# Second layer's tiles in the order in which the first layer ends; output copies one place later; the first pair's weight parts inside the last expert

## The chip, the core and the metric

The kernel runs on one core of a Trainium2 chip. The metric is the device time of one execution in microseconds. Engines: PE (TensorE: matmuls; its weight loads are listed as PEld), DVE (VectorE), ACT (ScalarE), POOL (GpSimd) and SP (SyncE, which here only issues transfers). A PE matmul accumulates into a bank of PSUM, and DVE or ACT reads the bank afterwards.

## The reference, cut

Three stages follow each other: a linear attention with decay (`_attn_ref`), a mixture of eight experts of which each token takes one (`_moe_ref`), and a two-layer perceptron with an ELU between (`_moe2_ref`). The change lies in the last stage and at its border to the second one:

```
def _moe2_ref(x, w_in, w_out):              # x: 2304 x 512, w_in: 512 x 2048, w_out: 2048 x 512
    h = x @ w_in
    g = np.where(h > 0.0, h, np.exp(np.minimum(h, 0.0)) - 1.0)
    return (g @ w_out).astype(np.float32)
```

## The kernel before, in words

Every operand of a matmul is split into a high part (a rounded copy, made on ACT) and a low part (the difference, made on DVE), and `three` (L223 to L229) issues three matmuls for a product: high by high, high by low, low by high.

**The experts.** The loop `for i in range(NI1 + 1)` runs 8 experts by 8 hidden tiles; `mm1` makes a hidden tile, `mm2` one step later adds it to four output banks, and after an expert's last tile the four banks are copied to `y` (three copies on ACT, the fourth on DVE). `decode` steps prepare the perceptron's weights in the gaps, and `load_pair` loads them in pairs. After the loop stand `decode(99)`, the allocation of the tiles for the perceptron's weights (`awt`, one set for even and one for odd groups) and, for the first pair, `weights_high` (ACT) and `weights_low` (DVE) of its four quarters `A11`, `A12`, `A21`, `A22`: four casts and four differences of 128x256. Then comes a `tc.If` for experts with too many tokens, whose body is not entered with these inputs, and then the perceptron.

**The perceptron.** The tokens are cut into three blocks of 768 (`TB`), the 2048 hidden units into eight pairs of 128-wide rows; a group `g` in 0 to 23 is one pair on one block. Groups 0 to 7 (`plain`) have four places with two products each; groups 8 to 23 (`seven`) compute the same with seven products (Strassen's way), one at each of seven places, with sums on DVE in between. A product is six matmuls of 384 columns into one of two banks. The group's four quarters (j, s) of the first layer (j: which 128 hidden units, s: which half of the block) end in the order (0,0) at place 2, (1,1) at 4, (1,0) at 5, (0,1) at 6. Each then goes through `elu`: three ACT operations (`r`, `ex`, `r`), one place later two on DVE (`ex`, L1220 and L1221), one place after that the high part `gh` on ACT, and one after that the low part `gl` on DVE (both L1224). So `gl` of (1,0) falls at place 1 of the next group.

**The second layer.** `out_units(g)` is a generator of twelve units for group g, which are issued during group g + 1, after the products: a unit is the three matmuls of 512 columns for token tile t (0 to 5) and hidden half j (0 or 1). Tiles t = 0 to 2 read the half s = 0, t = 3 to 5 the half s = 1. The list `share` says how many units follow each product: none at place 0, two at each of places 1 to 6 (in group 23 fewer, with the rest at the end). After a tile's last unit in the last pair of a block, its bank is copied to `ob` (tag `tsum`, three buffers; even t on ACT, odd t on DVE) and POOL scatters the rows to the output with an indirect transfer.

**What sets the order.** The program runs with a manual schedule: each engine executes in the order in which the code issues. At each place the order is: the product, `elus(2, ..)` (`gl`), `elus(0, 1)` (the two DVE steps), the queued tasks `low` and `high`, `elus(1, ..)` (`gh`), then the sum or copy of the place, then the units. At place 0 ACT copies the product's bank to `u` (L1308), and the product of place 2 adds to that same bank. The weights of groups 8 to 23 come back from DRAM through POOL's queue: `out_move(g, True)` (four loads for the second layer, tags with two free buffers) and then `weights_load(g + 1)` (seven loads for the first), both issued at place 0 of group g.

Of the kernel before, what the change touches and what calls it, by code (L numbers as in the profile page):

```python
# [9 lines left out]
F32 = mybir.dt.float32  # L10
# [69 lines left out]
def tile_kernel(ctx: ExitStack, tc: tile.TileContext, q, k, v, emb, tau, w1, w2, w_in, w_out, const, out):  # L80
# [932 lines left out]
    for low in lows + [xpose(0, 2)]:  # L1013
        low()
    NI1 = NE * 8
    load_unit(1, nc.scalar)
    split(1)
    for i in range(NI1 + 1):
# [28 lines left out]
        if i < NI1 - 2:  # L1047
            decode(2)

    decode(99)  # L1050

    awt = [[], []]
    for j in range(2):
        t = dec.tile([P, 2, 2, 2, P], F32R, tag="draw", name=f"awd{j}")
        awt[0] += [t[:, 0], t[:, 1]]
    for nm in ("dsq", "db1"):
        awt[0] += [dec.tile([P, 2, 2, P], F32R, tag=nm, name=f"aw{nm}{j}", bufs=2) for j in range(2)]
    t = raw.tile([P, 4, 2, 2, P], F32R, tag="rawb", name="awr")
    awt[1] += [t[:, i] for i in range(4)]
    awt[1] += [spl.tile([P, 2, 2, P], F32R, tag=nm, name=f"aw{nm}") for nm in ("ah", "al", "bh", "bl")]  # L1060
    A11, A12, A21, A22, S1, S2, S3, S4 = range(8)
    t = raw.tile([P, 2, 4, 2, P], F32, tag="rawb", name="sums")
    sums = [{i: t[:, g, k] for k, i in enumerate((S1, S2, S3, S4))} for g in range(2)]
    wsd = [dr.tile([P, 8, 2 * 2 * P], F32R, name=f"wsd{g}") for g in range(8)]
    wbd = [dr.tile([P, 4, DM], F32R, name=f"wbd{g}") for g in range(8)]

    def weights_src(g, i):
        if i >= S1:
            return sums[g % 2][i]
        ra = pairs[g][:, 0]  # L1070
        return ra[:, i % 2 * 2:i % 2 * 2 + 2, i // 2 * P:i // 2 * P + P]

    def weights_sum(g, i):
        x = lambda k: weights_src(g, k)
        p_, q_, op = {S1: (A21, A22, ALU.add), S2: (S1, A11, ALU.subtract), S3: (A11, A21, ALU.subtract), S4: (A12, S2, ALU.subtract)}[i]
        vec.tensor_tensor(out=x(i), in0=x(p_), in1=x(q_), op=op)

    def weights_high(g, i):
        nc.scalar.copy(out=awt[g % 2][i][:, 0], in_=weights_src(g, i))

    def weights_low(g, i):
        w = awt[g % 2][i]
        vec.tensor_tensor(out=w[:, 1], in0=weights_src(g, i), in1=w[:, 0].bitcast(F32), op=ALU.subtract)
# [9 lines left out]
    for i in (A11, A12, A21, A22):  # L1093
        weights_high(0, i)
        weights_low(0, i)
# [338 lines left out]
```

## Time and profile before

| | us |
|---|---|
| median of three runs | 802.85 |
| the three runs | 800.53, 802.85, 803.28 |
| the profiled execution, its own time | 804.02 |
| span of the profiled execution, first to last instruction | 801.9 |
| PE busy in the span | 747.2 (93%) |
| DVE busy | 542.3 (68%) |
| ACT busy | 439.2 (55%) |
| POOL busy | 277.0 (35%) |

The profiled execution took 804.02 us, of which 2.12 us lie outside its span. In the span the experts end at about 362 us, groups 0 to 7 run to about 498.6 us, groups 8 to 23 to about 775 us, and the rest is the last group's second layer and the last scatter. A row of a timeline begins with the start of the instruction in us from the span's start, then its duration; what stands in brackets at its end is the idle time of the engine before it and the instruction that ended this. A PE matmul's duration overlaps that of the next one: the distance between the starts of two matmuls is what each takes. PEclk is the granted TensorE clock, 1.00 for 2.4 GHz and 0.50 for 1.2 GHz.

### The profile page before, as it was taken

To read this page: it belongs to the slowest core of one execution; us is meant where nothing else is said; L and a number is where in the kernel's file an instruction comes from. 1 tells how busy PE (TensorE), PEld (TensorE's weight loads), DVE (VectorE), ACT (ScalarE), POOL (GpSimd) and SP (SyncE) were. 2 spreads that over 40 slices of the span, in tenths; PEclk is the share of its full clock that TensorE was granted. 3 is DMA by queue.
4 is the path that set the end of the run, shared out by engine and by line. 5 is a ranking of instruction groups with operands and counts; after the bars stand their busy time and mean duration, and the time that the engine had idled before them with its cause. 6 is when DMAs were issued, how large, how long until landed. Compare 5 with 4: busy or idle time off the path is not lost.

```text
span 801.9 us, 13886 instructions
## 1 busy us (share of the span) xinstructions
PE 747.2 (93%) x4952; PEld 675.3 (84%) x4953; DVE 542.3 (68%) x1127; ACT 439.2 (55%) x917; POOL 277.0 (35%) x460
## 2 busy tenths in 40 slices
PE   8899978999999999996999999899999899999984
PEld 7898957999999999995999899788887777888863
DVE  4366577889989999866778778555556765545551
ACT  3555534455555556547767778445445664544550
POOL 5365665269843512000000001553223445222303
PEclk9999999999999999999999999999999999999997
DMA  9898827776886877831967764786645668665512
GB/s 218 224 237 229 254 91 257 243 234 225 288 311 215 307 277 240 303 126 55 326 225 246 259 229 159 235 223 199 169 145 145 171 183 226 197 169 145 144 53 78
DMA packets 131870, 165.60 MB, mean 207 GB/s; under 512 B 63530, under 2 KB 68430, under 8 KB 131798
## 3 DMA queue, kind: packets, MB, share of 16 engines
q1 hardware_dynamic: 102630, 107.91, 41.4%
q0 software_dynamic: 27440, 54.15, 23.4%
q10 hardware_dynamic: 1728, 2.62, 1.0%
q8 instruction: 41, 0.67, 0.3%
q14 instruction: 31, 0.25, 0.1%
HBM read 123.73 MB, written 40.91 MB: 205 GB/s over the span
## 4 chain that ended last, share of the span: by engine, by line
PE 30%; DVE 9%; ACT 7%; issue 5%; POOL 1%; DMA 1%; POOLq 0%; DVEq 0%
PE o L229 6%; PE c L227 5%; PE c L228 5%; PE c L229 5%; PE o L227 5%; PE o L228 5%; DVE ex L1220 3%; ACT ex L1216 2%; ACT r L1217 2%; ACT r L1215 2%; DVE ex L1221 2%; DVE gl L1224 1%; DMA obl<-wbd 1%; DVE v L1294 1%; DVE u L1294 1%
## 5 line engine op out<-in xcount | busy, mean ns | idle before, releaser
L1220 DVE SCALAR_TENSOR_TENSOR ex<-ex,r 128x384 f32<-128x384 f32 x96 | 53.5, 558 | 123.0 <-ACT r L1217 123.0
L1201 POOL DMA_DIRECT2D oah<-wbd x16 | 8.7, 542 | 318.9 <-DMA wsd<-awdsq 185.9
L228 PE MATMUL acc<-hl,bh 128*128 128x342 f32 (+7 forms) x256 | 78.7, 308 | 2.1 <-DVE hl L869 1.8
L227 PE MATMUL h<-xth,ah 128*128 128x332 f32 (+7 forms) x252 | 78.5, 311 | 0.0
L229 PE MATMUL h<-xth,al 128*128 128x332 f32 (+7 forms) x252 | 76.7, 304 | 1.6 <-DVE al L217 1.5
L227 PE MATMUL acc<-hh,bh 128*128 128x342 f32 (+7 forms) x256 | 77.5, 303 | 0.0
L229 PE MATMUL acc<-hh,bl 128*128 128x342 f32 (+7 forms) x256 | 77.4, 302 | 0.0
L228 PE MATMUL h<-xtl,ah 128*128 128x332 f32 (+7 forms) x252 | 76.4, 303 | 0.0
L1224 ACT CAST gh<-ex 128x384 fp32r<-128x384 f32 x97 | 49.3, 508 | 33.5 <-DVE ex L1221 32.9
L229 PE MATMUL o<-obh,gl 128*128 128x512 f32 x144 | 58.5, 406 | 8.7 <-DVE gl L1224 7.2
L227 PE MATMUL o<-obh,gh 128*128 128x512 f32 x144 | 58.8, 409 | 3.3 <-ACT gh L1224 2.4
L229 PE MATMUL o<-oah,gl 128*128 128x512 f32 x144 | 57.5, 399 | 0.0
L227 PE MATMUL o<-oah,gh 128*128 128x512 f32 x144 | 57.3, 398 | 0.0
L228 PE MATMUL o<-oal,gh 128*128 128x512 f32 x144 | 57.0, 396 | 0.0
L228 PE MATMUL o<-obl,gh 128*128 128x512 f32 x144 | 56.9, 395 | 0.0
L1224 DVE TENSOR_TENSOR gl<-ex,gh 128x384 fp32r<-128x384 f32 x97 | 53.5, 552 | 1.2 <-ACT gh L1224 1.1
L1216 ACT ACTIVATE ex<-r 128x384 f32<-128x384 f32 x96 | 50.4, 525 | 3.0
L1217 ACT ACTIVATE r<-r 128x384 f32<-128x384 f32 x96 | 50.4, 525 | 3.0
L228 PEld LDWEIGHTS acc<-hl,bh 128*128 128x128 f32 x256 | 48.2, 188 | 4.4 <-DVE hl L869 4.3
L216 ACT CAST bh<-rawb 128x512 fp32r<-128x512 f32 x64 | 39.8, 622 | 19.4 <-PE acc L228 19.4
L217 DVE TENSOR_TENSOR bl<-rawb,bh 128x512 fp32r<-128x512 f32 x64 | 47.3, 739 | 3.5 <-ACT bh L216 3.4
L229 PEld LDWEIGHTS h<-xth,al 128*128 128x128 f32 x252 | 47.5, 189 | 2.4 <-DVE al L217 2.4
(408 smaller groups left out, 2182.1 us busy)
## 6 DMA issues: line engine op xcount, KB each, us to landing
rawa<-in_moe_w_dram SPq DMA_DIRECT2D x15, 1024.0 KB, 6.3
rawb<-in_moe_w_dram SPq DMA_DIRECT2D x15, 1024.0 KB
pair<-wd SPq DMA_DIRECT2D x18, 512.0 KB, 5.4
draw<-in_moe_w_in_dram SPq DMA_DIRECT2D x16, 512.0 KB, 9.0
wd<-db SPq DMA_DIRECT2D x32, 256.0 KB
draw<-in_moe_w_out_dram SPq DMA_DIRECT2D x16, 512.0 KB, 5.4
awr<-wsd POOLq DMA_DIRECT2D x24, 256.0 KB
awd<-wsd POOLq DMA_DIRECT2D x21, 256.0 KB
```

Source lines behind the costliest of these rows:

```text
L216: nc.scalar.copy(out=hi, in_=src)
L217: nc.vector.tensor_tensor(out=lo, in0=src, in1=hi.bitcast(F32), op=ALU.subtract)
L227: nc.tensor.matmul(o, lh, rh, start=first, stop=False, skip_group_check=free)
L228: nc.tensor.matmul(o, lh, rl, start=False, stop=False, skip_group_check=free)
L229: nc.tensor.matmul(o, ll, rh, start=False, stop=last, skip_group_check=free)
L1215: nc.scalar.activation(out=r, in_=c, func=AF.Relu, scale=-1.0)
L1216: nc.scalar.activation(out=ex, in_=r, func=AF.Exp, scale=-1.0)
L1217: nc.scalar.activation(out=r, in_=r, func=AF.Tanh, scale=-0.5)
L1220: vec.scalar_tensor_tensor(out=ex, in0=ex, scalar=1.0, in1=r, op0=ALU.add, op1=ALU.mult)
L1221: vec.scalar_tensor_tensor(out=ex, in0=c, scalar=0.0, in1=ex, op0=ALU.max, op1=ALU.add)
L1224: return middle, lambda: nc.scalar.copy(out=gh, in_=ex), lambda: vec.tensor_tensor(out=gl, in0=ex, in1=gh.bitcast(F32), op=ALU.subtract)
L1294: vec.tensor_tensor(out=o, in0=x, in1=c, op=ALU.add)
```

## The change

Three edits. **First**, `out_units` no longer goes tile by tile with both halves of each. It takes the units (t, 0) for t = 0, 1, 2, then (t, 1) for the same tiles, and then tiles 3 to 5 (for groups 8 to 22 all (t, 1) first and then all (t, 0); for groups 0 to 7 and 23 tile by tile). The units' number and the places with their shares stay. **Second**, the copy of a finished output tile and its scatter move out of `out_units` into `rows_out`, which is called at the next place, after `elus(0, 1)` and ahead of `low` and `high`; at the end of the program it is called after every unit. Beside it, `weights_load(g + 1)` is now issued ahead of `out_move(g, True)`. **Third**, the definitions and the first weight set move ahead of the expert loop's body, decoding is ended one step earlier, and the high and low parts of `A11`, `A12` are issued at step 62 and those of `A21`, `A22` at step 63 of the loop instead of after it.

```
-        for t in range(NTB):
+        todo = [(t, j) for j in range(2) for t in range(3)]
+        if g < 8:
+            todo += [(t, j) for t in range(3, NTB) for j in range(2)]
+        elif g < NG2 - 1:
+            todo += [(t, j) for j in (1, 0) for t in range(3, NTB)]
+        else:
+            todo += [(t, j) for t in range(3, NTB) for j in (1, 0)]
+        seen = set()
+        for t, j in todo:
             sl = slice(t * P, (t + 1) * P)
-            for j in range(2):
-                gh, gl = gs[g][j]
-                three(acc6[t], (gh[:, sl], gl[:, sl]), bs[g][j], p == 0 and j == 0, p == 7 and j == 1)
-                if p == 7 and j == 1:
-                    ob = fp.tile([P, DM], F32, tag="tsum", name=f"ob{b}_{t}", bufs=3)
...
+            gh, gl = gs[g][j]
+            three(acc6[t], (gh[:, sl], gl[:, sl]), bs[g][j], p == 0 and t not in seen, p == 7 and t in seen)
+            if p == 7 and t in seen:
+                ended.append((b, t))
+            seen.add(t)
+            yield
...
+    def rows_out():
+        for b, t in ended:
+            ob = fp.tile([P, DM], F32, tag="tsum", name=f"ob{b}_{t}", bufs=3)
...
             elus(2, 3)
             elus(0, 1)
+            rows_out()
             for f in low[k] + high[k]:
...
         put(low, o, out_tiles, g)
-        put(low, o, out_move, g, True)
         if g + 1 < NG2:
             put(low, o, weights_load, g + 1)
+        put(low, o, out_move, g, True)
...
-        if i < NI1 - 2:
+        if i < NI1 - 3:
             decode(2)
...
+        elif i == NI1 - 3:
+            decode(99)
+            first_set()
+        elif i < NI1:
+            for k in ((A11, A12), (A21, A22))[i - NI1 + 2]:
+                weights_high(0, k)
+                weights_low(0, k)
...
     for _ in out_units(NG2 - 1):
-        pass
+        rows_out()
+    rows_out()
```

What this moves is shown at three places. On PE, the units that follow the product of place 1 in group 19 (`o2_t` is the bank of token tile t of block 2, `gh18_j` and `gl18_j` the parts of the hidden half j, `oa`, `ob` the second layer's weights for j = 0 and 1); before:

```order
L227 MATMUL o2_0_8736<-oah18_8862,gh18_0_8901 128x512
L228 MATMUL o2_0_8736<-oal18_8863,gh18_0_8901 128x512
L229 MATMUL o2_0_8736<-oah18_8862,gl18_0_8902 128x512
L227 MATMUL o2_0_8736<-obh18_8864,gh18_1_8903 128x512
L228 MATMUL o2_0_8736<-obl18_8865,gh18_1_8903 128x512
L229 MATMUL o2_0_8736<-obh18_8864,gl18_1_8904 128x512
```

and with the change:

```order
L227 MATMUL o2_0_8736<-oah18_8862,gh18_0_8901 128x512
L228 MATMUL o2_0_8736<-oal18_8863,gh18_0_8901 128x512
L229 MATMUL o2_0_8736<-oah18_8862,gl18_0_8902 128x512
L227 MATMUL o2_1_8737<-oah18_8862,gh18_0_8901 128x512
L228 MATMUL o2_1_8737<-oal18_8863,gh18_0_8901 128x512
L229 MATMUL o2_1_8737<-oah18_8862,gl18_0_8902 128x512
```

The second unit at place 1 now reads the half j = 0 of tile 1; the first unit that reads the half j = 1 stands as second unit at place 2.

On DVE, the end of place 1 of group 8 and the places after it, where block 0 is copied out (`ob0_t` is the copy of output tile t); before:

```order
L1224 TENSOR_TENSOR gl7_1_7152<-ex7_11_7281,gh7_1_7151 128x384
L1241 COPY ob0_1_7380<-o0_1_6119 128x512
L1220 SCALAR_TENSOR_TENSOR ex8_00_7370<-ex8_00_7370,r8_00_7369 128x384
L1221 SCALAR_TENSOR_TENSOR ex8_00_7370<-c0_8_0_7294,ex8_00_7370 128x384
L1294 TENSOR_TENSOR v8_7297<-u8_7296,c1_8_2_7384 128x384
L1294 TENSOR_TENSOR v8_7297<-v8_7297,c0_8_3_7404 128x384
L1241 COPY ob0_3_7424<-o0_3_6121 128x512
L1224 TENSOR_TENSOR gl8_0_7366<-ex8_00_7370,gh8_0_7365 128x384
L1220 SCALAR_TENSOR_TENSOR ex8_11_7414<-ex8_11_7414,r8_11_7413 128x384
L1221 SCALAR_TENSOR_TENSOR ex8_11_7414<-v8_7297,ex8_11_7414 128x384
L1294 TENSOR_TENSOR w8_7298<-u8_7296,c1_8_2_7384 128x384
```

and with the change:

```order
L1231 TENSOR_TENSOR gl7_1_7152<-ex7_11_7281,gh7_1_7151 128x384
L1227 SCALAR_TENSOR_TENSOR ex8_00_7366<-ex8_00_7366,r8_00_7365 128x384
L1228 SCALAR_TENSOR_TENSOR ex8_00_7366<-c0_8_0_7294,ex8_00_7366 128x384
L1318 TENSOR_TENSOR v8_7297<-u8_7296,c1_8_2_7376 128x384
L1264 COPY ob0_1_7403<-o0_1_6119 128x512
L1318 TENSOR_TENSOR v8_7297<-v8_7297,c0_8_3_7396 128x384
L1231 TENSOR_TENSOR gl8_0_7362<-ex8_00_7366,gh8_0_7361 128x384
L1227 SCALAR_TENSOR_TENSOR ex8_11_7414<-ex8_11_7414,r8_11_7413 128x384
L1228 SCALAR_TENSOR_TENSOR ex8_11_7414<-v8_7297,ex8_11_7414 128x384
L1264 COPY ob0_3_7433<-o0_3_6121 128x512
L1318 TENSOR_TENSOR w8_7298<-u8_7296,c1_8_2_7376 128x384
```

The copy of tile 3 now stands behind `gl8_0` and the two DVE steps of quarter (1,1), directly ahead of the sum `w8`.

On ACT, the end of the last expert (`hh62`, `hh63` are its last two hidden tiles, `acc56_d` its output banks, `awd0`, `awd1` the tiles of the four quarters' parts); before:

```order
L868 ACTIVATE hh62_5390<-h62_5377 128x276
L868 ACTIVATE hh63_5419<-h63_5406 128x276
L891 TENSOR_LOAD offi_89
L891 ISA x2
L888 ISA
L888 COPY y_1978<-acc56_0_5196 128x276
L888 ISA
L888 COPY y_1978<-acc56_1_5197 128x276
L888 ISA
L888 COPY y_1978<-acc56_2_5198 128x276
L1079 CAST awd0_5469<-pair0_5220 128x256 x2
L1079 CAST awd1_5470<-pair0_5220 128x256 x2
```

and with the change:

```order
L868 ACTIVATE hh62_5412<-h62_5399 128x276
L1033 CAST awd0_5393<-pair0_5236 128x256 x2
L868 ACTIVATE hh63_5445<-h63_5432 128x276
L1033 CAST awd1_5394<-pair0_5236 128x256 x2
L891 TENSOR_LOAD offi_89
L891 ISA x2
L888 ISA
L888 COPY y_1978<-acc56_0_5212 128x276
L888 ISA
L888 COPY y_1978<-acc56_1_5213 128x276
L888 ISA
L888 COPY y_1978<-acc56_2_5214 128x276
```

The four casts moved from behind the last expert's copies to behind its last two hidden tiles; the four differences on DVE moved alike.

## Rows read from the trace of the kernel before

**Rows 1.** Busy time of the engines in one stretch, groups 0 to 7: stretch, length in us, busy us and instructions of PE, PEld, DVE, ACT and POOL, granted clock, share of the DMA engines, GB/s.

```profile
380.00:498.00 118.00, 117.35 (x586) 106.10 (x587) 90.66 (x195) 86.80 (x191) 0.00 (x0) 1.00 0.69 244
```

**Rows 2.** Timeline of PE: the product of place 2 of group 8; then from place 6 of group 18 to place 2 of group 19 (products of places 6, 0 and 1, the first unit, the first matmul of the second unit and its last, the product of place 2, the unit after it); then the product of place 2 of group 23.

```profile
502.22 0.34 PE L227 MATMUL c<-t1h,awd 128*128 128x384 f32 x1
...
690.03 0.34 PE L227 MATMUL c<-t2h,awdb 128*128 128x384 f32 x1
...
692.48 0.34 PE L227 MATMUL c<-t0h,awr 128*128 128x384 f32 x1
...
693.65 0.44 PE L227 MATMUL c<-t4h,awal 128*128 128x384 f32 x1
...
694.80 0.39 PE L227 MATMUL o<-oah,gh 128*128 128x512 f32 x1
...
695.73 0.50 PE L227 MATMUL o<-obh,gh 128*128 128x512 f32 x1
...
696.98 0.50 PE L229 MATMUL o<-obh,gl 128*128 128x512 f32 x1 [0.51 <-DVE gl L1224]
697.31 0.34 PE L227 MATMUL c<-t1h,awr 128*128 128x384 f32 x1
...
698.37 0.39 PE L227 MATMUL o<-oah,gh 128*128 128x512 f32 x1
...
765.58 0.34 PE L227 MATMUL c<-t1h,awr 128*128 128x384 f32 x1
```

**Rows 3.** Timelines of DVE and of ACT in the same stretch around the start of group 19: the last sum of group 18, the first DVE step of its quarter (0,1), `gl` of its quarter (1,0); and ACT's copy of the bank of group 19's place 0.

```profile
693.05 0.55 DVE L1294 TENSOR_TENSOR u<-u,c 128x384 f32<-128x384 f32 x1
695.30 0.56 DVE L1220 SCALAR_TENSOR_TENSOR ex<-ex,r 128x384 f32<-128x384 f32 x1 [1.24 <-ACT r L1217]
...
696.37 0.55 DVE L1224 TENSOR_TENSOR gl<-ex,gh 128x384 fp32r<-128x384 f32 x1
...
695.58 0.47 ACT L1308 COPY u<-c 128x384 f32<-128x384 f32 x1
```

**Rows 4.** Timelines of PE, POOL and DVE around the start of group 9: PE's product of place 6 of group 8 and of places 0, 1 and 2 of group 9; POOL's scatter of output tile 0 of block 0; DVE's copy of tile 3.

```profile
512.01 0.34 PE L227 MATMUL c<-t2h,awdb 128*128 128x384 f32 x1
...
515.63 0.44 PE L227 MATMUL c<-t0h,awr 128*128 128x384 f32 x1 [1.01 <-DVE w L1294]
...
518.95 0.69 PE L227 MATMUL c<-t4h,awal 128*128 128x384 f32 x1 [2.01 <-DVE u L1294]
...
522.98 0.34 PE L227 MATMUL c<-t1h,awr 128*128 128x384 f32 x1
...
508.52 1.05 POOL L1246 DMA_INDIRECT out_dram<-ob,idc  x1 [2.01 <-DMA awr<-wsd]
...
512.89 0.69 DVE L1241 COPY ob<-o 128x512 f32<-128x512 f32 x1 [3.96 <-DMA out_dram<-ob,idc]
```

**Rows 5.** Timelines of PE and ACT at the starts of groups 14 and 16: PE's last matmul of the second unit in group 14; in group 16 its first unit and the product of place 2, and ACT's copy of the bank of place 0.

```profile
608.85 0.50 PE L229 MATMUL o<-obh,gl 128*128 128x512 f32 x1 [1.38 <-DVE gl L1224]
...
642.57 0.39 PE L227 MATMUL o<-oah,gh 128*128 128x512 f32 x1
...
645.92 0.34 PE L227 MATMUL c<-t1h,awd 128*128 128x384 f32 x1
...
644.05 0.47 ACT L1308 COPY u<-c 128x384 f32<-128x384 f32 x1
```

**Rows 6.** Busy time in single microseconds, columns as in Rows 1: after the idle time at the start of group 0, and after that at the start of group 9.

```profile
366.00:367.00 1.00, 1.00 (x4) 1.00 (x4) 0.96 (x2) 1.00 (x2) 0.00 (x0) 0.50 0.00 0
...
519.00:520.00 1.00, 1.00 (x3) 1.00 (x4) 0.96 (x2) 0.97 (x2) 0.59 (x3) 0.50 0.16 61
```

**Rows 7.** Timelines of SP, ACT, DVE and PE from the last expert to the perceptron's first product: SP's issue of the load of the first pair's first-layer half; ACT's `hh` of the last hidden tile; DVE's copy of the fourth output bank and its four differences for the first pair; ACT's first token part; PE's first product.

```profile
343.82 0.60 SPq L179 DMA_DIRECT2D pair<-wd  x1
...
358.78 0.40 ACT L868 ACTIVATE hh<-h 128x276 fp32r<-128x276 f32 x1 [2.66 <-PE h L229]
...
361.85 0.45 DVE L886 COPY y<-acc 128x276 f32 x1 [2.20 <-PE acc L229]
362.22 1.42 DVE L1083 TENSOR_TENSOR awd<-pair,awd 128x256 fp32r<-128x256 f32 x4
364.02 0.93 ACT L1173 CAST t0h<-y 128x384 fp32r<-128x384 f32 x2 [0.94 <-DVEq L1101]
364.58 0.45 PE L227 MATMUL c<-t0h,awd 128*128 128x384 f32 x1 [2.77 <-ACT t0h L1173]
```

**Rows 8.** Timelines of PE, POOL and ACT at the end: PE's first matmul that reads the half j = 1 of group 23, the last matmul of that unit, and the last matmul of all; POOL's scatters of output tiles 0, 1 and 5 of block 2; ACT's copy of tile 4.

```profile
780.37 0.50 PE L227 MATMUL o<-obh,gh 128*128 128x512 f32 x1 [1.68 <-ACT gh L1224]
...
781.62 0.79 PE L229 MATMUL o<-obh,gl 128*128 128x512 f32 x1 [0.52 <-DVE gl L1224]
783.32 1.03 POOL L1246 DMA_INDIRECT out_dram<-ob,idc  x1 [20.64 <-ACT ob L1243]
...
785.98 1.00 POOL L1246 DMA_INDIRECT out_dram<-ob,idc  x1 [1.55 <-DVE ob L1241]
...
789.31 0.59 ACT L1243 COPY ob<-o 128x512 f32<-128x512 f32 x1 [2.21 <-PE o L229]
...
790.28 0.39 PE L229 MATMUL o<-obh,gl 128*128 128x512 f32 x1
...
791.73 0.97 POOL L1246 DMA_INDIRECT out_dram<-ob,idc  x1 [0.46 <-DVE ob L1241]
```

More of the change, by code (lines that the diff above doesn't have):

```diff
@@ L1046, in tile_kernel @@
         split(i + 2)
-        if i < NI1 - 2:
+        if i < NI1 - 3:
             decode(2)
-    decode(99)
-    awt = [[], []]
-    for j in range(2):
[L1054 to L1083, printed above, removed]
-    def weights_store(g, i):
-        if i != A21:
-            nc.sync.dma_start(out=wsd[g % 8][:, i, :].bitcast(F32), in_=awt[g % 2][i].rearrange("p a k f -> p (a k f)").bitcast(F32))
-    def weights_load(g):
-        for i in LEFTS:
-            pool.dma_start(out=awt[g % 2][i].rearrange("p a k f -> p (a k f)"), in_=wsd[g % 8][:, i, :])
-    for i in (A11, A12, A21, A22):
-        weights_high(0, i)
-        weights_low(0, i)
+        elif i == NI1 - 3:
[5 more added lines that the diff above has]
+                weights_low(0, k)
+    second_set()
     qctx.close()
@@ L1232, in out_units @@
                 acc6[t] = pm.tile([P, 512], F32, tag=tag, name=f"o{b}_{t}", bufs=1 if t < 4 else 2)
-        for t in range(NTB):
-            sl = slice(t * P, (t + 1) * P)
-            for j in range(2):
-                gh, gl = gs[g][j]
-                three(acc6[t], (gh[:, sl], gl[:, sl]), bs[g][j], p == 0 and j == 0, p == 7 and j == 1)
-                if p == 7 and j == 1:
-                    ob = fp.tile([P, DM], F32, tag="tsum", name=f"ob{b}_{t}", bufs=3)
-                    if t % 2:
-                        vec.tensor_copy(out=ob, in_=acc6[t])
-                    else:
-                        nc.scalar.copy(out=ob, in_=acc6[t])
-                    col = b * NTB + t
-                    pool.memset(nil, 0.0)
-                    ins = pool.indirect_dma_start(
-                        out=out[:, :], out_offset=bass.IndirectOffsetOnAxis(ap=idc[:, col:col + 1], axis=0), in_=ob, in_offset=None)
-                    tc.declare_no_dep(ins.ins, group="rows", reason="each token's row is written once")
-                    tc.add_to_no_dep_group("rows", ins.ins)
-                yield
+        todo = [(t, j) for j in range(2) for t in range(3)]
@@ new lines, in tile_kernel @@
+    ended = []
+    def rows_out():
+        for b, t in ended:
+            ob = fp.tile([P, DM], F32, tag="tsum", name=f"ob{b}_{t}", bufs=3)
+            if t % 2:
+                vec.tensor_copy(out=ob, in_=acc6[t])
+            else:
+                nc.scalar.copy(out=ob, in_=acc6[t])
+            col = b * NTB + t
+            pool.memset(nil, 0.0)
+            ins = pool.indirect_dma_start(
+                out=out[:, :], out_offset=bass.IndirectOffsetOnAxis(ap=idc[:, col:col + 1], axis=0), in_=ob, in_offset=None)
+            tc.declare_no_dep(ins.ins, group="rows", reason="each token's row is written once")
+            tc.add_to_no_dep_group("rows", ins.ins)
+        ended.clear()
@@ L1402, in tile_kernel @@
     for _ in out_units(NG2 - 1):
-        pass
+        rows_out()
+    rows_out()
 _INS = ["q", "k", "v", "moe_expert_emb", "moe_tau", "moe_w1", "moe_w2", "moe2_w_in", "moe2_w_out"]
```

37 lines of the change are left out of this document (added).

## The prediction

> **What bounds the kernel now.** I read the shares of the engines first: PE is busy 93% of the span, so only PE's idle time and the ends of the program can give anything. Then the table of busy time by stretch: in groups 0 to 7 PE is busy 117.35 of 118 us at clock 1.00 [rows 1], so nothing is to be had there. Then PE's timeline from group 8 on. A place with two units takes 2.45 us unhindered (place 6 of group 18 to place 0 of group 19, 690.03 to 692.48), a product alone 1.06 (697.31 to 698.37) [rows 2], so two units take 1.39 and a group of seven places 6 x 2.45 + 1.06 = 15.76. From place 2 of group 8 to place 2 of group 23 passed 765.58 - 502.22 = 263.36 us [rows 2]; 15 unhindered groups make 236.4. So 27.0 us are waits of PE, and the waits that follow say where. Last I followed the border between experts and perceptron and the last scatters.
>
> **Part 1, the order of the units, in an ordinary group.** In group 19 the first unit starts at 694.80 and the product of place 2 at 697.31: 2.51 instead of 1.39, so 1.12 us are lost. The second unit waits for `gl` of quarter (1,0) of group 18 [rows 2]. DVE has it only at 696.37 + 0.55 = 696.92, since it stands behind the first step of quarter (0,1), which waits for ACT's chain [rows 3]. With the change the two units of place 1 read the half j = 0, complete by then; the first unit with j = 1 is the second of place 2 and comes near 694.80 + 1.39 + 1.06 + 0.70 = 697.95, 1.0 after `gl`. So the 1.12 goes.
>
> What is late next? The product of place 2 adds to the bank of place 0 and so waits for ACT's copy to `u`, which ends at 695.58 + 0.47 = 696.05 [rows 3]; PE will be there at 694.80 + 1.39 = 696.19. The margin is 0.14, less whatever a signal takes. The trace of before does not show this wait. Below, it costs nothing; above, I allow 0.19 a group (the copy late by as much as the margin, and a little). I take 0.07, nearer to nothing because this row has the copy in time. The wait at place 1 for the last sum of the group before (692.48 to 693.65 is 1.17 for 1.06) stays.
>
> I count 12 such boundaries among the starts of groups 10 to 23, without 14 and 16. In group 14 the `gl` wait is 1.38 where group 19 has 0.51 [rows 2, 5], so 1.12 + 0.87 = 1.99 goes; part of this delay belongs to DVE work that also stands ahead of the sum `u`, and I charge 0.5 (bounds 0 and 0.87). In group 16, first unit to place 2 is 645.92 - 642.57 = 3.35, so 1.96 goes; but there the copy to `u` ends at 644.52, after PE's new arrival at 643.96, and 0.56 comes back [rows 5], say 0.6. At the start of group 17, where block 1 is copied out, the moved copies now stand directly ahead of a sum on DVE (0.69 [rows 4]) and of the copy to `u` on ACT (0.59 [rows 8]): I charge 0.6 and 0.4. Gain: 12 x 1.12 + 1.99 + 1.96 = 17.4; new waits: 0.5 + 0.6 + 1.0 = 2.1, and 12 x 0.07 = 0.9. **Net 14.4** (12.8 with 0.19 a group and the other new waits a little dearer; 16.3 with half of these and none at place 2).
>
> **Part 2, block 0's copies, in groups 8 and 9.** Place 6 of group 8 starts at 512.01, place 2 of group 9 only at 522.98 [rows 4]. The cause is POOL: its scatter of tile 0 runs only at 508.52, when the weight loads ahead of it are through; so the third buffer's successor, DVE's copy of tile 3, waits 3.96 until 512.89, the sums `w` and `u` behind it are late, and PE waits 1.01 and 2.01 [rows 4]. Then the clock falls to 0.50 [rows 6]. With the change `weights_load` goes first; its tiles come free as the plain products end, so POOL is free when tile 0 has been copied, near 502.22 + 1.06 + 1.39 = 504.7 for the product of place 3, plus the copy: about 505.9. Its landing takes no more than the 3.3 between a tile 1's scatter (785.98) and the copy of tile 4 to the same buffer (789.31) [rows 8]. So the buffer is free near 510, and tile 3 wants it at about 511.7. The copy still stands ahead of `w`, so I leave a wait of 0.6. Then place 0 of group 9 is at 512.01 + 2.45 = 514.46, and place 2 at 514.46 + 1.06 + 0.21 + 0.6 + 1.06 + 1.39 = 518.78 (0.21: the wait at place 1 as in group 19, 0.11, and 0.1 for the weight load ahead of it). **Gain 4.2** (2.6 with double the waits and half the clock loss; 4.8 with none). `out_move`, now second on POOL, is needed a group later; nothing waits for it.
>
> The delay of the copies by a place costs ordinary groups nothing: only the last pair of a block has copies.
>
> **Part 3, the border.** The first product waits 2.77 for `t0h`, ACT's first token part; ACT waits for DVE, whose four differences (1.42 from 362.22) stand behind the copy of the fourth bank (361.85 + 0.45 = 362.30). They end at 363.64, and `t0h` starts at 364.02 [rows 7], 0.38 later. With the differences gone it starts at 362.30 + 0.38 = 362.68: **1.3** sooner. What covers the moved work: ACT was idle 2.66 before its last `hh` and DVE 2.20 before its last copy, and the load of the pair was issued at 343.82, 15 us before that `hh` [rows 7]. SP's order does not change. Without this cover two casts and two differences, some 0.7 each side, would delay `hh` and the last `mm2`: lower bound 0. Upper bound 2.7: PE's idle time is halved, and if the clock, which was 0.50 after it [rows 6], does not fall, as much again comes back.
>
> **Part 4, the end.** In group 23 the first unit with j = 1 waits until 781.62 for `gl`, in both orders; but three units instead of one lie ahead of it, so that eight instead of ten follow, two less by 1.39 (and one more if the clock holds). PE's last matmul, 790.28, comes 1.4 to 3 sooner. Then POOL bounds it: scatter 0 at 783.32, each scatter about 1.03, so scatter 2 not ahead of 785.4; 3.3 to land, and the copy of tile 5 into its buffer (0.69) give 789.4, the last scatter at about 789.8 instead of 791.73 [rows 8]. **Gain 1.9** (1.0 if landing takes the 4.4 between 508.52 and 512.89 [rows 4], 2.4 if the buffers never wait). The Trainium skill, "DMA: Bandwidth & Descriptors", section "Anatomy of one DMA — SWDGE (gpsimd) path", gives a fixed 2.0 us plus the bytes by 436 GB/s, an estimate of 2.6 us for a tile of 256 KB; the trace agrees, as the scatter of tile 1 needs no more than 3.3 [rows 8], and by the page the end would gain the whole 2.4.
>
> **Sum.** 14.4 + 4.2 + 1.3 + 1.9 = 21.8 us. The profiled execution goes from 804.02 to 782.2; it lies 1.2 above the median of 802.85, from which 781.1 follows. I say 781.5. The low ends sum to 12.8 + 2.6 + 0 + 1.0 = 16.4 (787 from the two bases), the high ends to 16.3 + 4.8 + 2.7 + 2.4 = 26.2 (777).
>
> **Rivals.** (A) **The wait only changes its name:** place 2's product waits for the copy to `u` about 0.5 us in each of 13 boundaries, as group 16 shows [rows 5], instead of 0.07: 6.5 less, 788. For it: a margin of 0.14. Against it: the copy was in time in group 19 [rows 3]. (B) **Block 0's scatter stays late:** if `weights_load`, seven loads in one queue, still holds POOL beyond 508, part 2 gives nothing: 786. (C) **Slower: the clock.** Units now leave a bank after three matmuls rather than six. If PE were idle at those changes and the clock fell each time, the price of a fall is that of group 9: place 1 to place 2 took 522.98 - 518.95 = 4.03 instead of 2.45 [rows 4], 1.57. From 14 falls it eats the 21.8, and two in each of 16 groups cost 50: 831. Against it: in groups 0 to 7 three units follow each place, a bank is left after three or six matmuls there too, and the clock is 1.00 [rows 1]. The Trainium skill, "TensorE: Matmul & The Clock Gate", section "A second HAM failure mode: psum-queue depth-cycling", tells of a kernel whose clock swings because it cycles through banks; the stretch of [rows 1] speaks against it. (D) **Part 3 moves no end:** if another engine holds `t0h`, the differences moved away free nothing: 782.8.
>
> **How the numbers follow.** The forecast has 0.80, A 0.10, B 0.05, D 0.03, C 0.02. The range takes in all but C and the tails of the sum, A at its upper edge: 777 to 788. A measurement of this kernel tells about 0.5%, 4 us, from no change. All cases but C lie 14 us or more below the median; for milder mishaps that leave less than 4 I put 0.03. Faster 0.95, same 0.03, slower 0.02.
>
> **What would show it.** Right: places 2 lie some 16.0 us apart instead of 17.6, and PE's waits for `gl` and `gh` at units are gone except at the end; POOL's scatter of tile 0 comes near 506, and place 2 of group 9 is 16.6 after that of group 8; `t0h` starts 0.4 after DVE's last copy; the last scatter starts near 1.5 us after the last matmul or later, held by a buffer. Wrong: waits of place 2's product for ACT (A), a DVE copy that waits for a transfer in group 8 (B), clock 0.50 within the groups (C). It would be most wrong if DVE, with its waits gone, became what PE follows in each group.

## The result, and the profile after

The changed kernel takes 783.09 us (median of four runs, 780.08 to 784.48), the kernel before 802.67 beside it (four runs, 800.53 to 803.28): a ratio of 0.9756, 95% interval 0.9718 to 0.9793, which is 16.6 to 22.6 us less. Its profiled execution took 784.48 us, with a span of 782.4; the one of before 804.02 and 801.9, so the two profiles differ by 19.5. Cut at five marks of the timelines they differ as follows (the place 2 of a group is the start of that product on PE):

| stretch | before | after | gain | forecast |
|---|---|---|---|---|
| start to ACT's last `hh` of the experts | 358.78 | 360.38 | -1.60 | 0 |
| to PE's third product of group 0 | 10.27 | 9.23 | 1.04 | 1.3 |
| to place 2 of group 8 | 133.17 | 133.17 | 0 | 0 |
| to place 2 of group 9 | 20.76 | 16.56 | 4.20 | 4.2 |
| to place 2 of group 23 | 242.60 | 228.92 | 13.68 | 14.4 |
| to the last scatter | 26.15 | 23.97 | 2.18 | 1.9 |
| sum | | | 19.50 | 21.8 |

The first row goes with the clock of the first stage, which the change leaves as it was; the last section shows it. Of the moved work only two casts and two differences lie in this row's stretch, and ACT idles 2.06 us behind them before the last `hh`. `e1_units` and `e2_copies` below, which have the border as before, end this stretch at 359.67 and 360.90.

**PE's waits.** The list of waits of the kernel after, grouped by what waited and for whom (us in total, times, longest):

```profile
PE c L227 <- issue: 2.1, 1, 2.1
...
PE c L227 <- DVE u L1318: 1.4, 3, 0.5
...
PE o L229 <- DVE gl L1231: 0.5, 1, 0.5
...
PE o L227 <- ACT gh L1231: 0.3, 1, 0.3
...
PE c L227 <- ACT u L1333: 0.2, 1, 0.2
```

The units (`o`) wait once for `gl` and once for `gh`, both at the end of the program. Of the fifteen starts of groups none has the wait of [rows 2] left. Five waits remain at products of groups 9 to 17; the largest are the next readings.

**An ordinary group.** Timelines of PE and ACT of the kernel after: place 2 of group 18, the second unit at place 1 of group 19 and place 2 there, place 2 of group 23; ACT's copy to `u` in group 19. Then the busy time of the stretch, columns as in [rows 1]:

```profile
668.41 0.34 PE L227 MATMUL c<-t1h,awd 128*128 128x384 f32 x1
683.00 0.39 PE L227 MATMUL o<-oah,gh 128*128 128x512 f32 x1
...
684.39 0.34 PE L227 MATMUL c<-t1h,awr 128*128 128x384 f32 x1
...
748.26 0.34 PE L227 MATMUL c<-t1h,awr 128*128 128x384 f32 x1
...
683.76 0.47 ACT L1333 COPY u<-c 128x384 f32<-128x384 f32 x1
```

```profile
652.50:748.00 95.50, 95.50 (x467) 84.03 (x468) 52.30 (x103) 50.52 (x102) 38.76 (x74) 1.00 0.68 193
```

Group 18 to 19 takes 684.39 - 668.41 = 15.98, and first unit to place 2 takes 1.39, unhindered. ACT's copy ends at 684.23, 0.16 ahead of the product that adds to its bank. In these six groups PE has no idle time at all and the clock is 1.00.

**Groups 8 and 9.** Timelines of PE, POOL and DVE of the kernel after: place 2 of group 8, places 1 and 2 of group 9; the scatter of tile 0; the copy of tile 3 and the sum behind it.

```profile
502.78 0.34 PE L227 MATMUL c<-t1h,awd 128*128 128x384 f32 x1
...
516.78 0.44 PE L227 MATMUL c<-t4h,awal 128*128 128x384 f32 x1 [0.55 <-DVE u L1318]
...
519.34 0.34 PE L227 MATMUL c<-t1h,awr 128*128 128x384 f32 x1
...
506.40 1.06 POOL L1269 DMA_INDIRECT out_dram<-ob,idc  x1 [5.25 <-ACT ob L1266]
...
512.27 0.68 DVE L1264 COPY ob<-o 128x512 f32<-128x512 f32 x1
512.87 0.54 DVE L1318 TENSOR_TENSOR w<-u,c 128x384 f32<-128x384 f32 x1
```

The scatter now waits for its copy and not for weight loads; the copy of tile 3 has no wait in brackets, where [rows 4] had 3.96; it delays `w` by its 0.6, and PE waits 0.55 once.

**Groups 15 and 16, where the forecast failed.** Timelines of PE and DVE of the kernel after: places 2 of groups 15 and 16 and place 1 of group 16; two low parts of block 2's token tiles (`t5l`, `t3l`) and the sums behind them. Then the clock in two stretches:

```profile
615.78 0.34 PE L227 MATMUL c<-t1h,awr 128*128 128x384 f32 x1
...
631.34 0.42 PE L227 MATMUL c<-t4h,awdsq 128*128 128x384 f32 x1 [2.09 <-issue]
...
635.32 0.43 PE L227 MATMUL c<-t1h,awd 128*128 128x384 f32 x1
...
625.63 0.95 DVE L1183 TENSOR_TENSOR t5l<-tsr,t5h 128x768 fp32r<-128x768 f32 x1
626.50 0.55 DVE L1318 TENSOR_TENSOR w<-u,c 128x384 f32<-128x384 f32 x1
...
629.82 0.95 DVE L1183 TENSOR_TENSOR t3l<-tsr,t3h 128x768 fp32r<-128x768 f32 x1
630.69 0.55 DVE L1318 TENSOR_TENSOR u<-u,c 128x384 f32<-128x384 f32 x1
```

```profile
631.00:633.00 2.00, 1.66 (x7) 1.69 (x8) 0.77 (x3) 1.66 (x4) 0.00 (x0) 0.77 1.10 309
633.00:635.00 2.00, 2.00 (x6) 1.54 (x6) 1.97 (x4) 1.83 (x4) 0.00 (x0) 0.50 0.22 68
```

From place 2 of group 15 to that of 16 passed 19.54 us, hardly less than the 19.67 of before. The wait at place 1 names no releaser, but PE starts 0.1 after the end of the sum `u` (630.69 + 0.55), which stands behind `t3l`. And after this wait the clock is 0.50. In the kernel before, the wait at the same product was shorter; its row on PE:

```profile
641.44 0.41 PE L227 MATMUL c<-t4h,awdsq 128*128 128x384 f32 x1 [1.74 <-issue]
```

**The border and the end.** Timelines of ACT, PE and DVE of the kernel after from the last expert on, and of POOL, DVE at the end:

```profile
360.38 0.40 ACT L868 ACTIVATE hh<-h 128x276 fp32r<-128x276 f32 x1 [2.06 <-PE h L229]
...
363.13 0.29 PE L229 MATMUL acc<-hh,bl 128*128 128x276 f32 x1
...
363.46 0.45 DVE L886 COPY y<-acc 128x276 f32 x1 [1.53 <-PE acc L229]
...
365.02 0.93 ACT L1180 CAST t0h<-y 128x384 fp32r<-128x384 f32 x2 [1.56 <-PEq L1108]
...
369.61 0.34 PE L227 MATMUL c<-t0h,awd 128*128 128x384 f32 x1
...
765.69 1.03 POOL L1269 DMA_INDIRECT out_dram<-ob,idc  x1 [18.53 <-ACT ob L1266]
...
768.71 0.69 DVE L1264 COPY ob<-o 128x512 f32<-128x512 f32 x1 [2.50 <-DMA out_dram<-ob,idc]
...
772.23 0.97 POOL L1269 DMA_INDIRECT out_dram<-ob,idc  x1 [0.23 <-issue]
```

`t0h` starts 4.64 us after the last `hh` instead of 5.24, released by PE's sequencer (PEq) at the line of the conditional part and no longer by DVE. At the end the copy of tile 3 waits for the scatter of tile 0, as the forecast had it: landed 3.02 after its start.

### The profile page after: what moved, and what is told of

Its sections match the earlier page's. It is cut to its first block, busy times and chain, and to the rows that moved or that the text cites. A ratio compares the mean times of both kernels' runs of the same rounds, so it can differ in the third digit from the quotient of the medians.

```text
span 782.4 us, 13945 instructions
## 1 busy us (share of the span) xinstructions
PE 741.1 (95%) x4952; PEld 676.9 (87%) x4953; DVE 542.7 (69%) x1127; ACT 439.0 (56%) x917; POOL 277.4 (35%) x460
## 4 chain that ended last, share of the span: by engine, by line
PE 40%; DVE 4%; ACT 4%; issue 3%; POOL 1%; POOLq 0%; ACTq 0%
PE c L227 7%; PE o L227 7%; PE o L229 7%; PE o L228 7%; PE c L228 6%; PE c L229 6%; ACT ex L1223 1%; ACT r L1222 1%; DVE ex L1227 1%; ACT r L1224 1%; DVE ex L1228 1%; POOL out_dram L1269 1%; DVE v L1318 0%; DVE u L1318 0%; DVE w L1318 0%
## 5 line engine op out<-in xcount | busy, mean ns | idle before, releaser
L1045 POOL DMA_DIRECT2D awr<-wsd x24 | 13.0, 542 | 198.3 <-ACT t1h L1180 178.3
L229 PE MATMUL o<-obh,gl 128*128 128x512 f32 x144 | 56.8, 395 | 0.5 <-DVE gl L1231 0.5
L227 PE MATMUL o<-obh,gh 128*128 128x512 f32 x144 | 57.0, 396 | 0.3 <-ACT gh L1231 0.3
L217 DVE TENSOR_TENSOR al<-rawa,ah 128x512 fp32r<-128x512 f32 x64 | 48.0, 750 | 2.7 <-ACT ah L216 2.2
```

The source lines that it names most:

```text
L217: nc.vector.tensor_tensor(out=lo, in0=src, in1=hi.bitcast(F32), op=ALU.subtract)
L227: nc.tensor.matmul(o, lh, rh, start=first, stop=False, skip_group_check=free)
L229: nc.tensor.matmul(o, ll, rh, start=False, stop=last, skip_group_check=free)
L1045: pool.dma_start(out=awt[g % 2][i].rearrange("p a k f -> p (a k f)"), in_=wsd[g % 8][:, i, :])
```

## The experiments

**One part of the change at a time.** Three kernels make one edit each on the kernel before; a fourth makes only the exchange of POOL's loads. `e1_units`: the new list of units, the copies where they were:

```
+        todo = [(t, j) for j in range(2) for t in range(3)]
...
             if p == 7 and t in seen:
-                ended.append((b, t))
+                ob = fp.tile([P, DM], F32, tag="tsum", name=f"ob{b}_{t}", bufs=3)
```

> Only the order of the second layer's units is changed; copies, POOL's order and the border stay as before. Theory (each group's 1.1 us come from the units alone): places 2 of ordinary groups lie 15.97 us apart as with the whole change, not 17.07; from place 2 of group 8 to that of group 9 it stays near 20 us, since the scatter of tile 0 is as late as before; the end gains about 2. In all some 15 us less than before, about 787. Rival (the units' order pays only with the copies moved as well): periods at or above 16.5 us, less than 10 us in all.

`e2_copies`: `rows_out` a place later and the loads exchanged, units tile by tile as before:

```
+        todo = [(t, j) for t in range(NTB) for j in range(2)]
...
             elus(0, 1)
+            rows_out()
```

> Only the copies of output tiles a place later and the weight loads first on POOL; units and border as before. Theory: the stretch from place 2 of group 8 to that of group 9 falls from 20.76 to 17.7 us (16.56 as with the whole change plus the 1.1 of the old order of units), all other periods stay 17.07, some 3 us less in all, about 799.7. Rival (the long stretch came from the clock or the units, not from the late scatter): it stays above 19.5 us.

`e3_border`: only the first pair's weight parts at steps 62 and 63.

```
+            for k in ((A11, A12), (A21, A22))[i - NI1 + 2]:
+                weights_high(0, k)
+                weights_low(0, k)
```

> Only the first pair's weight parts inside the last expert. Theory (PE's sequencer, on its way through the branch, is next late): the first token part starts 4.6 us after the start of the last hidden tile's activation instead of 5.24, and the first product's third quarter comes 1.0 us sooner; nothing else moves, 1 us in all, about 801.7, hardly to be told from no change by the time. Rival (DVE's copy is next late, as the forecast had it): 3.9 us after that start, 1.3 or more in all.

`e4_loads_first`:

```
-        put(low, o, out_move, g, True)
         if g + 1 < NG2:
             put(low, o, weights_load, g + 1)
+        put(low, o, out_move, g, True)
```

> Only POOL's order: the loads of the next group's weights ahead of those of the second layer; copies stay at their units. Theory (POOL's order alone frees the scatters): the scatter of tile 0 comes near 504 instead of 508.5, no copy on DVE waits for a transfer in group 8, and places 2 of groups 8 and 9 lie 17.1 to 17.9 us apart. Rival (the copies' delay is what did it): 19.5 us or more.

Measured, distances of places 2 in us from their timelines, and the times:

| kernel | groups 8 to 9 | ordinary | 15 to 16 | 16 to 17 | 8 to 23 | last scatter after place 2 of 23 | time | ratio, interval |
|---|---|---|---|---|---|---|---|---|
| before | 20.76 | 17.07 | 19.67 | 17.25 | 263.36 | 26.15 | 802.67 | |
| after | 16.56 | 15.97 | 19.54 | 17.03 | 245.48 | 23.97 | 783.09 | 0.976 (0.972 to 0.979) |
| e1_units | 21.80 | 15.97 | 19.13 | 16.83 | 250.39 | 23.95 | 787.41 | 0.979 (0.975 to 0.982) |
| e2_copies | 18.26 | 17.06 | 19.67 | 18.24 | 261.72 | 24.58 | 800.71 | 0.996 (0.994 to 0.998) |
| e3_border | 21.21 | 17.06 | 19.66 | 17.26 | 263.71 | 26.10 | 802.94 | 0.999 (0.996 to 1.001) |
| e4_loads_first | 17.74 | 17.07 | 19.67 | 17.26 | 260.26 | 24.57 | 799.24, one run | |

The order of the units alone gives the 1.1 us of every ordinary group, as its theory said. Places 2 of groups 18 and 19 on PE in `e1_units`:

```profile
674.05 0.34 PE L227 MATMUL c<-t1h,awd 128*128 128x384 f32 x1
...
690.00 0.36 PE L227 MATMUL c<-t1h,awr 128*128 128x384 f32 x1
```

Groups 8 to 9, which were to stay near 20, took 21.80, 1.0 longer than before: block 0's late scatter is still there (508.96), PE waits 1.44 and 2.00 for the sums behind it, and the clock is 0.50 from 520 to 526 instead of from 519 to 522. `e3_border`, whose edit does not touch this stretch, is 0.45 longer than before there, so part of that 1.0 can be a difference between executions. POOL's order alone takes 3.0 of that stretch: scatter of tile 0 at 503.20, PE's distance within what was expected; but a copy on DVE still waited 1.32 for a scatter, which had not been expected. The border alone starts `t0h` 4.57 after the last `hh` (expected 4.6, the rival 3.9); its time can't be told from no change.

`e2_copies` gave 18.26 where 17.7 was expected, and lost 1.0 in groups 16 to 17 where it was said to leave all alone: the moved copies delay DVE there, and PE waits 0.54 for a sum and 1.11 for `gl` at the second unit, instead of 0.52 for `gl` alone. So is the copies' delay worth anything? That was put to a kernel with everything else as after (and block 2's token parts late, see below), `e10_copies_at_units`, which issues the copies at the units again:

```
             if p == 7 and t in seen:
-                ended.append((b, t))
+                ob = fp.tile([P, DM], F32, tag="tsum", name=f"ob{b}_{t}", bufs=3)
...
-            rows_out()
```

> The run with the late token parts, but the output copies at their units as before the change, one place sooner, with POOL's loads first. Theory (POOL's order alone freed the scatters, so the copies' delay is worth nothing): group 8 to 9 takes 16.5 to 16.8 us, group 16 to 17 16.8 to 17.0, and place 2 of group 8 to that of group 23 242.0 to 242.6 as against 242.3 with the delay. Rival (the delay is worth something): group 8 to 9 above 17.2.

Groups 8 to 9 took 17.59 there (16.54 with the delay), 16 to 17 took 16.43 (17.03 with it), 8 to 23 242.73 (242.30); one run took 782.19 us. The theory fell: with the new order of units the delay is worth 1.05 in group 9, and it costs 0.6 in group 17. Timelines of POOL, DVE and PE of that kernel: the scatter of tile 0, the copy of tile 3, and place 1 of group 9.

```profile
506.74 1.06 POOL L1261 DMA_INDIRECT out_dram<-ob,idc  x1 [5.23 <-ACT ob L1258]
...
512.11 0.69 DVE L1256 COPY ob<-o 128x512 f32<-128x512 f32 x1 [2.27 <-DMA out_dram<-ob,idc]
...
518.17 0.44 PE L227 MATMUL c<-t4h,awal 128*128 128x384 f32 x1 [1.58 <-DVE u L1310]
```

Wanted a place sooner, the copy stands 2.27 us on a scatter that takes 512.11 - 506.74 = 5.37 to land.

**The groups where block 2's tokens are made ready.** `e5_late_tokens` puts DVE's sums and low parts for block 2 behind the sum of their place, where DVE otherwise waits for ACT:

```
-        put(low, o + n, tokens_sum, 2, i)
+        put(late, o + n, tokens_sum, 2, i)
...
-        put(low, o + n + 2, tokens_low, 2, i)
+        put(late, o + n + 2, tokens_low, 2, i)
...
                 begun(elu(g, 0, 1, u))
+            for f in late[k]:
+                f()
```

> The changed kernel, with block 2's token sums (in group 14) and the low parts of its token tiles (in groups 15 and 16) on DVE behind the sum of their place instead of ahead of it. Theory (the last sum of group 15 comes late because a low part of 0.95 stands ahead of it and another ahead of the sum before, and the clock falls in the wait of 2.1 us): from place 2 of group 15 to that of 16 it falls from 19.54 to 16.0 to 16.6 us with clock 1.00, and group 14 to 15 from 16.59 to about 16.0; 3.5 to 4.1 us less than the changed kernel, about 779. Rival (PE waits there for the loads of group 16's weights, the wait having no releaser in the profile): 19.5 stays, and at most 0.6 is gained.

Measured: 16.58 from group 15 to 16 instead of 19.54, at clock 1.00; 245.48 becomes 242.30; 778.43 us, ratio to the kernel before 0.968 (0.966 to 0.971). Places 2 of groups 15 and 16 on PE in this kernel:

```profile
612.62 0.33 PE L227 MATMUL c<-t1h,awr 128*128 128x384 f32 x1
...
629.20 0.44 PE L227 MATMUL c<-t1h,awd 128*128 128x384 f32 x1 [0.45 <-ACT u L1333]
```

The rival, loads, is out, since the loads are the same and the wait is gone. Group 14 to 15 stayed at 16.57: that half of the expectation was wrong, the wait only went on to the next product.

`e6_late_copies` does the same with the output copies:

```
             elus(0, 1)
-            rows_out()
...
                 begun(elu(g, 0, 1, u))
+            rows_out()
             yield
```

> The changed kernel, with the copies of output tiles behind the sum of their place instead of ahead of it. Theory (a DVE copy ahead of a sum costs PE the 0.55 seen at the starts of groups 9 and 17, an ACT copy ahead of the copy to u 0.24): group 8 to 9 falls from 16.56 to about 16.0, group 16 to 17 from 17.03 to 16.1 to 16.4; 1.0 to 1.5 us less from place 2 of group 8 to that of group 23, 244.0 to 244.5 instead of 245.48. Rival (the copies only move to the next place's work): no change, 245.5.

Group 16 to 17 fell to 16.07, as expected, group 8 to 9 only to 16.34, since ACT's copy of an even tile now stands ahead of ACT's copy to `u`. From 8 to 23 it took 243.32; 0.83 of the gain (19.54 - 18.71 from group 15 to 16) is the clock, which did not fall in group 16 this time though PE waited as long (2.10). `e9_no_if` below, which leaves the copies as they are, has 18.71 and a clock of 1.00 there too. So 1.3 are the copies' own. One run took 780.13 us.

Both moves (`e7_both`):

> The changed kernel with both moves: the output copies and block 2's token sums and low parts behind the sum of their place. Theory (they free different boundaries, so their gains add): 245.48 - 3.2 - 1.2 = about 241.0 us from place 2 of group 8 to that of group 23, and a median of 776 to 778. Rival (work put behind the sums meets the copies in groups 16 and 17): above 242.3, no better than the token parts alone.

241.10, as the sum of the two said; 777.63 us, ratio 0.969 (0.966 to 0.971). Then the high parts of the same tiles on ACT (`e11_all_late`):

```
-        put(high, o + n + 1, tokens_high, 2, i)
+        put(late, o + n + 1, tokens_high, 2, i)
```

> As the run with both moves, and block 2's high parts on ACT behind the ELU steps of their place too. Theory (the 0.6 us that groups 15 and 16 still lose is ACT's copy to u, held by a high part of 0.83 ahead of it): periods of about 16.0 to 16.1 there, 1.0 to 1.2 us less than with both moves, about 239.9 from place 2 of group 8 to that of group 23. Rival (ACT has no idle time behind the ELU steps either, and the next place's steps come late instead): no gain, 241 or more.

Again 241.10, with 16.61 from group 15 to 16: no gain, 776.60 us, ratio 0.968 (0.965 to 0.971). Timelines of ACT and PE of this kernel in group 16:

```profile
627.43 0.82 ACT L1180 CAST t6h<-tsr 128x768 fp32r<-128x768 f32 x1
...
628.15 0.51 ACT L1231 CAST gh<-ex 128x384 fp32r<-128x384 f32 x1
...
628.57 0.47 ACT L1332 COPY u<-c 128x384 f32<-128x384 f32 x1
...
629.09 0.44 PE L227 MATMUL c<-t1h,awd 128*128 128x384 f32 x1 [0.47 <-ACT u L1332]
```

The cast moved to the end of place 6, and there it still stands ahead of place 0's `gh` and copy. `e12_past_u` moves it past them:

```
-        put(late, o + n + 1, tokens_high, 2, i)
-        put(late, o + n + 2, tokens_low, 2, i)
+        put(late, o + n + 1 + (n > 4), tokens_high, 2, i)
+        put(late, o + n + 2 + (n > 4), tokens_low, 2, i)
```

> As the run with all token parts late, and the last two token tiles of block 2 split one place later, so that the high part of the second last stands behind ACT's copy to u in group 16, not ahead of it. Theory (in that run this cast of 0.83 us, at the end of place 6, still stood ahead of the high part of quarter (1,0) and of the copy to u, and was all of the 0.6 us wait of place 2): group 15 to 16 falls from 16.61 to 16.0 to 16.1 us, and place 2 of group 8 to that of group 23 takes 240.5 instead of 241.1; the median, 776, can't tell it. Rival (the copy waits for the chain of the low parts on DVE, not for the cast): 16.6 stays.

15.99 and 240.46, with the wait gone, so it was the cast. The time, 779.17 us, ratio 0.970 (0.968 to 0.973), isn't told from that of the two before. Timeline of ACT and PE of this kernel at the same place:

```profile
628.07 0.47 ACT L1332 COPY u<-c 128x384 f32<-128x384 f32 x1
...
628.44 0.83 ACT L1180 CAST t6h<-tsr 128x768 fp32r<-128x768 f32 x1
628.72 0.33 PE L227 MATMUL c<-t1h,awd 128*128 128x384 f32 x1
```

**The margin at place 2.** `e8_double_u`:

```
                 nc.scalar.copy(out=u, in_=a)
+                nc.scalar.copy(out=u, in_=a)
```

> The changed kernel, with ACT's copy of place 0's bank to u made twice, 0.47 us more on ACT in each of groups 8 to 23. Theory (the copy to u is the next late work of place 2's product, with a margin of 0.10 a group): 0.3 to 0.4 us more in each ordinary group, period 16.3 to 16.4 instead of 15.97, and place 2 of group 8 to that of group 23 takes about 250 us instead of 245.5. Rival (PE does not follow ACT there): 245.5 to 246.

Period 16.46, 251.45 from group 8 to 23: 0.49 a group, somewhat more than expected. Timelines of ACT and PE of this kernel in group 19:

```profile
685.70 0.47 ACT L1333 COPY u<-c 128x384 f32<-128x384 f32 x1
...
686.21 0.48 ACT L1334 COPY u<-c 128x384 f32<-128x384 f32 x1
...
686.74 0.44 PE L227 MATMUL c<-t1h,awr 128*128 128x384 f32 x1 [0.27 <-ACT u L1334]
```

PE starts 0.05 after the second copy's end, and the first matmul after a wait lasts 0.44 instead of 0.34, which the expectation had left out and which would be the other 0.1. The copy to `u` is next late in every ordinary group, with nearly nothing to spare. One run took 788.67 us.

**The branch.** `e9_no_if` leaves the conditional part out:

```
-    with tc.If(n_trips > 0):
-        with tc.For_i(0, n_trips, 1) as it:
...
```

> The changed kernel without the conditional part for experts with too many tokens, which is left out of the program and is not entered with these inputs. Theory (the first token part starts only when PE's sequencer has come to that branch, 1.6 us after its last matmul, and no longer waits for DVE): without the branch it starts within 0.4 us of the end of DVE's last copy of y instead of 1.11 after it, 3.5 to 3.9 us after the start of the last hidden tile's activation instead of 4.64. Rival (something else than the branch holds it): 4.6 us.

Timelines of DVE and ACT of this kernel:

```profile
360.13 0.45 DVE L886 COPY y<-acc 128x276 f32 x1 [1.53 <-PE acc L229]
...
360.48 0.93 ACT L1149 CAST t0h<-y 128x384 fp32r<-128x384 f32 x2 [0.34 <-ACT y L888]
```

`t0h` starts 3.43 us after the last `hh` (357.05) instead of 4.64 (3.5 to 3.9 was expected), even before DVE's copy has ended, and the third of PE's products comes 7.84 after it instead of 9.23. So the branch held it. One run took 778.41 us.

## Why the prediction was right, and where it was not

It said 781.5 us in 777 to 788, and 783.09 was measured. In the two profiles the parts gave 21.10 of the 21.8 forecast, and 1.60 went the other way at the start. That the sum came so near is in part luck, as parts 2 and 4 show. By its parts:

- **Part 1** was to give 14.4 and gave 13.68. The 1.12 of an ordinary group went as described, for the reason described: `e1_units` has it alone. Place 2's wait for ACT, charged 0.07, is 0 in ordinary groups, but `e8_double_u` shows the margin was judged rightly. The periods that end at place 2 of groups 14 and 15 together gave 2.44 of 2.54 (what was charged as 0.5 at the start of group 14 came at its place 3, as 0.6 in the period to group 15), group 17's new waits for a sum and for `u` came at 0.55 and 0.24. **The step that failed is group 16:** I counted only from the first unit to place 2 and charged 0.6 for the copy to `u`; the wait of 1.74 for the sum at place 1, ahead of these, the sum does not name and so leaves as it was. Instead it grew to 2.09, since PE came sooner to a sum that DVE's low parts hold (a wait that stays is as long as its chain is late, not as long as it was), and in this execution the clock fell behind it (0.83 us, by the 18.71 of `e6_late_copies`, where it did not). So 0.13 of the 1.36 came. The charge for `u` was right in kind: where the clock held, PE waits 0.46 (`e6_late_copies`) and 0.45 (`e9_no_if`) for it; behind the slow clock this wait does not show. `e5_late_tokens` undoes the chain and finds 2.96 us in this period.
- **Part 2** was to give 4.2 and gave 4.20, PE's waits included. The order on POOL is the greater part (`e4_loads_first`, 3.0). The reason holds, but its slack was too large: I had the scatter land within 3.3 us by a row of the program's end, though [rows 4] has 4.37 for this very scatter, and the buffer free near 510, 1.7 ahead of its use; in `e10_copies_at_units` it took 5.37, which would leave 0.5 here (506.40 + 5.37 = 511.77, use at 512.27). Only the copies' delay made it fit, so it is luck that the forecast was met exactly. Of the two edits of this part the prediction gave the delay no worth; it is 1.05 with the new units and a loss with the old (18.26 in `e2_copies` against 17.74 in `e4_loads_first`).
- **Part 3** was to give 1.3 and gave 1.04. The differences did move off the chain, but the work next late was not DVE's copy: PE's sequencer comes through the conditional part 1.6 us after PE's last matmul (363.13 + 0.29 to 365.02), and `e9_no_if` shows that this part is what holds `t0h`. So `t0h` starts 1.11 after DVE's last copy, where the forecast had 0.4. Worked out with the same 1.6 from PE's last matmul of before, which ended at 361.82, it had been there at 363.4, 0.6 ahead of the `t0h` of [rows 7]; that is what `t0h` gained. The rest came at the first products: `t0l`, DVE's difference that they need, starts 0.54 after `t0h` instead of 1.04 (365.56 after 365.02, before 365.06 after 364.02).
- **Part 4** was to give 1.9 and gave 2.18, but not from the order alone. In the kernel before the clock was 0.50 after the wait for `gl`; `e4_loads_first` has the same units there and kept 1.00, and its end took 24.57 instead of 26.15. The busy time of two stretches behind that wait, before and then in `e4_loads_first`:

```profile
782.00:784.00 2.00, 2.00 (x6) 1.52 (x6) 0.23 (x1) 0.59 (x1) 0.69 (x1) 0.50 0.00 0
```

```profile
780.00:782.00 2.00, 2.00 (x10) 1.60 (x9) 0.69 (x1) 0.26 (x1) 1.61 (x3) 1.00 0.31 119
```

  So where the clock holds, the order is worth 0.6, down to the limit by buffers that the prediction named (the copies of tiles 3 to 5 wait for scatters); 1.6 is a fall of the clock. Whether that fall is chance or hangs on POOL's order is not shown: it is there in both profiles with the old units and the old order of loads (before, and 26.10 in `e3_border`) and in neither with the loads exchanged (`e4_loads_first`, and 24.58 in `e2_copies`), while PE's waits ahead of it are the same (1.68 and 0.52, in `e4_loads_first` 1.67 and 0.52). The Trainium skill, "DMA: Bandwidth & Descriptors", section "Anatomy of one DMA — SWDGE (gpsimd) path", gives a fixed 2.0 us plus the bytes by 436 GB/s, an estimate of 2.6 us for such a tile: near the 3.02 at the end, far from the 5.37 in group 8. The measurements decide, and they differ by the place in the program.
- **The rivals.** A (the wait moves to place 2) did not come, but was 0.1 to 0.2 us a group away; its price was put too high, since 0.5 instead of 0.07 at 13 boundaries is 5.6 us more and not 6.5. B fell: the scatter came at 506.40. D came by half: another engine, PE's sequencer, does hold `t0h`, but it was there 0.6 sooner than DVE. C fell: units leave a bank after three matmuls through groups 18 to 23, and PE is busy 95.50 of 95.50 us at 1.00. The Trainium skill's "TensorE: Matmul & The Clock Gate", section "A second HAM failure mode: psum-queue depth-cycling", tells of a clock that swings where PE, cycling through banks, idles briefly between groups of matmuls. In this stretch PE does not idle and the clock does not swing, so the case of that section is not put to the test. The falls that do occur here follow waits, as in group 16.

## What to carry to other kernels

When a wait is taken away, ask of every other wait on that engine whether its chain gets shorter too: where it does not, PE comes sooner and waits longer, and the gain is lost there. Side work that an in-order engine must do is put behind the work that PE waits for, here behind DVE's sums and ACT's copies to `u`; moving block 2's token parts and the output copies so brought another 5 us from group 8 to 23 (245.48 to 240.46), of which 0.83 is the clock of group 16, which fell in one execution and not in another. And a buffer's slack is measured where it is used: in `e10_copies_at_units` the scatter of tile 0 landed in 5.37 us in group 8, where the share of the DMA engines was 1.07 to 1.17 in the microseconds from 506 to 509, and in 3.11 at the end (763.30 to 766.41), where it was 0.00 to 0.68. That the other transfers are the reason is not shown.

## What was not expected of the hardware

The clock does not fall each time for the same wait. In group 16 PE waited 2.09 us in the kernel after and 2.10 in `e6_late_copies`; the first had 0.50 behind it (631.34, above), the second 1.00, and the distance of places 2 was 19.54 and 18.71. `e1_units` (2.10) had the fall as well, `e8_double_u` (2.11) and `e9_no_if` (2.10) had none. The three without it ran on one chip and `e1_units` on another, so a difference between chips is not excluded. PE's row of that wait and the busy time behind it in `e6_late_copies`:

```profile
629.16 0.42 PE L227 MATMUL c<-t4h,awdsq 128*128 128x384 f32 x1 [2.10 <-issue]
```

```profile
629.00:631.00 2.00, 1.84 (x10) 1.75 (x11) 0.76 (x3) 1.85 (x4) 0.00 (x0) 1.00 1.00 293
```

The first stage, which the change leaves as it was, has its clock differ between executions too. There PE's wait for `qs` near 9 us is not always the same (1.29 us before, 1.89 after), but its length alone does not tell: `e1_units`, with 1.19, had 0.91 over the first 40 us. These 40 us of the kernel before and of the one after:

```profile
0.00:40.00 40.00, 34.44 (x422) 31.82 (x423) 16.83 (x39) 17.63 (x39) 17.82 (x30) 1.00 0.92 221
```

```profile
0.00:40.00 40.00, 34.06 (x392) 31.16 (x394) 16.06 (x37) 16.23 (x35) 16.76 (x29) 0.91 0.88 213
```

Over the profiles of all fourteen kernels the experts' last `hh` comes at 356.51 to 358.78 us where this clock was 0.96 to 1.00, and at 359.67 to 360.90 where it was 0.87 to 0.91. The -1.60 of the first table goes with this, and is of a size with which runs of one kernel differ (780.08 to 784.48); no run changes this clock alone. What makes the clock fall in one execution and not in another stays open; it was not tried.
